# Attention and a state-space convolution on one core: the start of the program in another order, and one planner constant moved from 26 to 26.7

## The chip, the cores and the metric

One core of a Trainium2 chip runs the whole program. The metric is the device time of one execution in microseconds (us). Five engines work side by side, each through its own list of instructions: TensorE (PE, with its weight loads as PEld), VectorE (DVE), ScalarE (ACT), GpSimd (POOL) and SyncE (SP, which issues most DMAs; ACT issues a few).

## The reference

```python
x = A_x                                            # 1 x 2048 x 512, bf16
g = sigmoid((x * gate_w).sum(-1, keepdims=True))
# a: attention, 32 heads of 16
qkv = (x @ wqkv).reshape(B, S, 3, H, Dh)           # -> q, k, v
p = softmax(einsum("bhqd,bhkd->bhqk", q, k) * Dh**-0.5)
a = einsum("bhqk,bhkd->bhqd", p, v).reshape(B, S, D) @ wo
# b: a diagonal state-space convolution over 2048 steps, 128 states a channel
dt = exp(log_dt)[:, None]
P  = exp((dt * (A_re + 1j * A_im))[:, :, None] * arange(L))
K  = einsum("dn,dnl,dn->dl", Cc, P, dt * Bc).real  # 512 x 2048
b  = causal_conv(x, K) + x * Dskip
return g * a + (1 - g) * b
```

## The kernel before, in words

**Attention.** The scores of one head, 128 keys and 512 queries are a tile; there are 2048 tiles. Three tiles make a group, so that there are 683 groups. `qk(g)` multiplies a group's keys (`KT`) by the queries (`Qm`) into one of two PSUM buffers, `SC[0]` and `SC[1]`, in turn. `ex(g)` is one instruction of ACT that takes the exponential of the buffer into `ET` (or `EX`, for the last groups). For some groups VectorE takes the third tile: one instruction turns the scores into the bits of an approximate exponential (`DZ`), and after four such tiles, called a set, three instructions add constants to these bits (`DU`), whose average is the exponential. ACT's instruction in such a group has 1024 columns and not 1536. `pv` multiplies the exponentials by the values (`VE`) into the PSUM bank `OA`. A fourth PSUM buffer, `MB`, serves all else in turn: the other projections, the convolution's kernel (`T`, `Z`) and its products (`U`, `H`), and the output's projection.

**The order of the work.** Every engine's list is written ahead by a planner in Python (`Prog` with a time for each engine and a cost for each instruction, `Sched` with threads of waiting work). The loop over the groups emits `ex(g)` and `qk(g+1)`, and then fills the time of PE, DVE and SP up to ACT's time with work of the threads that is ready. So whatever changes the planner's times early moves all that follows. Where PE's products of a group fall short of `want` columns, the planner adds products with a tile of zeros (`wm`); they compute nothing. Whether VectorE takes a set is settled in `decide`, which asks `win`:

```python
def win(x):
    slow = done() < KA + (x - KX) / KB
    return next((w for w, (lo, hi, _, gap, *_) in enumerate(WIN) if lo <= x < hi and x >= plan["x"] + (SL if slow else gap)
                 and len(sets) <= (min(x, XR) - RX) / RATE + max(x - XR, 0) / RATE2), None)
```

Here `x` is the group and `done()` counts the finished blocks, of 16, of the convolution's kernel. Where these are behind the line with the slope 1/`KB`, sets come at least `SL` = 9 groups apart. `decide` also asks for an idle share of VectorE by the planner's times.

**The front.** Before the loop stands a fixed order. ACT's queue issues the loads of `x0n` (the first 512 rows of x), `ldt` (log_dt), and the first 128 columns of `Wq` and `Wk`; SP's queue the rest. PE runs nine products of zeros, transposes `x0n` with an identity (16 products; SC and MB to `xT`, four casts, one on ACT and three on DVE), runs `WARM` = 6 products of zeros into OA, and projects the first 512 queries (four products into OA) and the first 512 keys (four into SC[0]). DVE masks the queries (`Qm`) and casts the keys (`KT`). Then `qk(0)`, whose three tiles all have the first 128 keys, and the first exponential follow. Beside this, ACT computes `dt` = exp(`ldt`), and from `bn` = `AimT` x `dt` (DVE) a sine and a cosine (`sb_`, `cb`), for which it loads another table, and the table of the exponential again behind them.

All products are recorded at line 701, the helper `mm`; the exponentials stand at L961, DZ at L982, DU at L996.

Of the kernel before, what the change touches and what calls it, by code (L numbers as in the profile page):

```python
# [10 lines left out]
AF = mybir.ActivationFunctionType  # L11
ALU = mybir.AluOpType

P = 128
S = 2048
D = 512
# [16 lines left out]
FILL = 1550  # L33
FILL2 = 1550
OVER = .3
REST = (14, 0, 1792, 425)
# [21 lines left out]
KX = 100  # L58
SL = 9
YQ = 0  # L60
KB = 26
RX = 100
RATE2 = 5.3
XR = 560
# [72 lines left out]
class Prog:  # L137
# [113 lines left out]
    def op(self, eng, fn, R=(), W=(), c=.1, lat=.085, a=0, cfg=None):  # L251
        if self.cap is not None:
            self.cap.append((self.op, (eng, fn, R, W), dict(c=c, lat=lat, a=a, cfg=cfg)))
            return
        if cfg is not None:
            if cfg != self.cfg:
                c += TURN[cfg]
            self.cfg = cfg
        self.act += a
        self.log.append((self.op, self.q, (eng, fn, R, W)))  # L260
        deps = self._deps(eng, R, W)
        i = self.cnt[eng]
        at = self.tm[eng]
        for s, k in deps.items():
            at = max(at, self.fin[(s, k)] + (.03 if s == eng else .05))
        if eng == "PE" and len(self.pt) + 1 >= self.edge():
            at = max(at, self.land())
        self.tm[eng] = at + c
        if eng == "DVE":
            self.busy += c  # L270
        self.fin[(eng, i)] = at + c + lat
        self.cnt[eng] += 1
        w = self._record(eng, fn, deps, eng, i, R, W)
        if eng == "PE":
            b = self.edge()
            self.pt += [at] * (2 + max(w - 1, 0))
            if len(self.pt) > b:
                self.av.append(max(self.pt[b - LEAD] + F1, self.av[-1] + F2))
        return at + c + lat
# [406 lines left out]
def record(nc, p, B, ins):  # L686
    KT, Qm, VE, ET, OT, ON, Rz = (B[n] for n in ("KT", "Qm", "VE", "ET", "OT", "ON", "Rz"))
    OnT = {3: B["OnT3"]}
    OA, MB = B["OA"], B["MB"]
    SC = [B["SC0"], B["SC1"]]  # L690
    sch = Sched(p)
    op, dma = p.op, p.dma
# [6 lines left out]
    def mm(out, lhsT, rhs, R, W, start=True, stop=True, pos=None, c=MM, a=512, cfg="F"):  # L699
        kw = {} if pos is None else dict(tile_position=pos)  # L700
        op("PE", lambda t: t.matmul(out(), lhsT(), rhs(), start=start, stop=stop, skip_group_check=True, **kw), R, W,  # L701
           c=c, lat=.15, a=a, cfg=cfg)
# [80 lines left out]
    def proj_mm(kind, idx, c, bank, q4, wide=False):  # L783

        b, off, sl = bank
        w = B["Wk" if kind == "K" else "Wq"]
        strips(wide, lambda p, n: b(off, [[1, 512]], p, n), lambda p, n: w(q4 * D + 128 * idx + p, [[1, n]]), lambda: xT(q4 * S + 512 * c, [[1, 512]]),
               [xk(c, q4), (w, idx > 0)], [(b, sl, ('p', kind, idx, c))], q4 == 0, q4 == 3)

    def proj_ev(kind, idx, c, bank):  # L790
        b, off, sl = bank
        if kind == "K":
            o, at, ky = KT, idx * S + 512 * c, (idx, c)
        elif c + idx:
            o, at, ky = B["Qs"], idx % 2 * 512, idx % 2
        else:
            o, at, ky = B["Q"], 0, 0
        op("DVE", lambda v: v.tensor_copy(o(at, [[1, 512]]), b(off, [[1, 512]])), [(b, sl, ('p', kind, idx, c))],  # L798
           [(o, ky)], c=.62)
# [139 lines left out]
    def qk(g):  # L939
        sc = SC[g % 2]  # L940
        n = len(slots(g))
        for i, s in enumerate(slots(g)):
            q, j, b, kt, pi = at_slot(s)
            mm(lambda i=i: sc(512 * i, [[1, 512]]),
               lambda j=j, pi=pi, kt=kt: KT(pi * S + 128 * kt, [[1, 128]], 32 * j, 32),
               lambda j=j, b=b: Qm(512 * (b % 2), [[1, 512]], 32 * j, 32),
               [(KT, (pi, kt // 4)), (Qm, (b % 2, j), b)], [(sc, k, g) for k in (range(min(n, 2)) if i == 0 else [i])], pos=(32 * j, 0),
               c=QUAD if i == 0 else 0, a=128, cfg="R")
            if i == 0 and n == 3 and g % 2 == 0 and sch.now is not None:
                jz = 6 - sum(tiles[s] % 4 for s in slots(g))  # L950
                zero(zbank(), 512, (32 * jz, 0), 32, 128, 0, 128, "R")
# [93 lines left out]
    def key(*ns):  # L1045
        return [(B[n], 0) for n in ns]
# [643 lines left out]
            sch.mark(f"qm{b}")  # L1690


    mb, oa = (MB, 0, 0), (OA, 0, 0)
    for q4 in range(4):
        sc = SC[1] if q4 < 3 else MB
        off = 512 * (q4 % 3)
        sl = q4 % 3
        for i in range(4):
            mm(lambda sc=sc, off=off, i=i: sc(off + 128 * i, [[1, P]]), lambda q4=q4, i=i: x0n(D * i + P * q4, [[1, P]]),
               lambda: idb(0, [[1, P]]), [(x0n, 0), (idb, 0)], [(sc, sl, 'x0')], c=.11)  # L1700
        R, W = [(sc, sl, 'x0')], [(xT, (0, q4))]
        if q4 == 1:
            op("ACT", lambda v, sc=sc, off=off, q4=q4: v.copy(xT(q4 * S, [[1, 512]]), sc(off, [[1, 512]])), R, W, c=.58)
        else:
            op("DVE", lambda v, sc=sc, off=off, q4=q4: v.tensor_copy(xT(q4 * S, [[1, 512]]), sc(off, [[1, 512]])), R, W, c=.62)
    op("ACT", lambda a: a.activation(B["dt"](0, [[1, D]]), B["ldt"](0, [[1, D]]), AF.Exp), key("ldt"), key("dt"), c=.6)
    tt("DVE", full("bn"), full("AimT"), full("dt"), ALU.mult, key("AimT", "dt"), key("bn"), F5)
    op("ACT", lambda a: a.activation(B["sb_"](0, [[1, D]]), B["bn"](0, [[1, D]]), AF.Sin), key("bn"), key("sb_"), c=1.9)
    op("DVE", lambda v: v.scalar_tensor_tensor(B["ba"](0, [[1, D]]), B["bn"](0, [[1, D]]), -1.0, B["bn"](0, [[1, D]]), ALU.mult, ALU.max), key("bn"), key("ba"), c=F5)
    op("ACT", lambda a: a.activation(B["cb"](0, [[1, D]]), B["ba"](0, [[1, D]]), AF.Sin, scale=-1.0,  # L1710
                                     bias=hpi(0, [[1, 1]])), key("ba") + [(hpi, 0)], key("cb"), c=.6)
    for k in range(WARM):
        mm(lambda: OA(0, [[1, 512]]), lambda: wm(0, [[1, 128]]), lambda: wm(0, [[1, 512]]), [(wm, 0)], [(OA, 0, "warm")])
    for q4 in range(4):
        proj_mm("Q", 0, 0, oa, q4, True)
    for q4 in range(4):
        proj_mm("K", 0, 0, (SC[0], 0, 0), q4, True)
    op("DVE", lambda v: v.tensor_scalar(Qm(0, [[1, 512]]), OA(0, [[1, 512]]), msk(0, [[1, 1]]), None, ALU.mult),
       [(OA, 0, ('p', "Q", 0, 0)), (msk, 0)], [(Qm, (0, j), 0) for j in range(4)], c=.66)
    proj_ev("K", 0, 0, (SC[0], 0, 0))  # L1720
    decide(0)
    qk(0)
    proj_ev("Q", 0, 0, oa)
# [17 lines left out]
    for g in range(NG):  # L1741
        p.q = g
        for i in range(2 if g in vec else len(slots(g))):
            if held[g] + i in ring:
                sch.force(f"pv{ring[held[g] + i] // 4}")
            ring[held[g] + i] = tiles[3 * g + i]
        ex(g)
        sch.mark(f"g{g}")
        sch.mark(f"blk{at_slot(3 * g)[2]}")
        if g + 1 < NG:  # L1750
            decide(g + 1)
            need(g + 1)
            if g - 1 in vec:
                sch.force(f"bits{g - 1}")
            sc = SC[(g + 1) % 2]
            while lack >= 256 and bare:
                n = 512 if lack >= 512 else 256
                for j in range(4):
                    zero((sc, [(sc, 0, ("z", g + 1))]), n, (0, 32 * j), 128, 32, n * ZCOL if j == 0 else 0, n // 4, "C", True)
                lack -= n  # L1760
                bare -= 1
            lack += p.act
            qk(g + 1)
            if g + 1 in vec:
                i = sets[vec[g + 1][0]]["old"]
                if i is not None:
                    sch.force(f"dvp{i}")
                sch.add(bits(g + 1), 0)
        t = p.tm["ACT"]
        want = (FILL if g < REST[3] else FILL2) * (t - t0) / 1.335 + min(max(lack, -256), 768)  # L1770
        t0 = t
        sch.rest = g < REST[3] and g % REST[0] < REST[1]
        if sch.rest:
            want = max(want, REST[2])
        sch.fill(t, t + OVER, want)
        lack = want - p.act
        p.act = bare = 0
        while lack >= 256 and p.tm["PE"] < t + OVER and g < NG - 1:
            z = zbank()
            if z is None:  # L1780
                bare = BARE
                break
            n = 512 if lack >= 512 else 256
            for j in range(4):
                zero(z, n, (0, 32 * j), 128, 32, n * ZCOL if j == 0 else 0, n // 4, "C")
            lack -= n
        p.act = 0
# [71 lines left out]
```

## Time and profile before

| | |
|---|---|
| time, median of 3 runs | 786.94 us (786.87 to 787.43) |
| the profiled execution's own time | 787.2 us |
| its span | 785.4 us |
| ACT busy | 768.4 us (98%) |
| DVE busy | 748.7 us (95%) |
| PE busy | 689.5 us (88%) |
| first exponential starts | 11.92 us |
| last exponential ends | 776.56 us |

Times within the profile count from the span's start. Some 1.8 us of the profiled time lie outside its span. A row of the timeline merges like instructions that follow each other: start, length, engine, line, what is written and read, and how many. A line of the chain of waits gives the share of the span that each engine holds on the path that ended last.

### The profile page before, as it was taken

How to read it: one execution, taken by the hardware profiler on the slowest of the kernel's cores; microseconds unless marked ns; L12 is line 12 of the kernel's file. 1: busy time of each engine (PE TensorE's matmuls, PEld its weight loads, DVE VectorE, ACT ScalarE, POOL GpSimd, SP SyncE). 2: the span in 40 equal slices, each digit the busy share in tenths (PEclk: the TensorE clock that was granted, in tenths of full speed). 3: DMA queues.
4: the chain of work that ended last, by engine and by line, in shares of the span. 5: the costliest groups of instructions: out<-in, count | busy, mean ns of one | idle time of the engine just before them, and what ended most of it. 6: DMA issues, size and time to landing. Idle time of an engine off the chain costs nothing.

```text
span 785.4 us, 31633 instructions
## 1 busy us (share of the span) xinstructions
PE 689.5 (88%) x14177; PEld 295.3 (38%) x14177; DVE 748.7 (95%) x1307; ACT 768.4 (98%) x694; POOL 11.5 (1%) x21
## 2 busy tenths in 40 slices
PE   7787778788778999989999899989999999889997
PEld 3233332222224544445444455443444444322222
DVE  7999998999999999999999999999999999899996
ACT  7999999999999999999999999999999999999996
POOL 5000000000000000000000000000000000000000
PEclk9999999999999999999999999999999999999999
DMA  9544212302002677674776664775665588721101
GB/s 201 90 108 89 62 40 92 116 31 59 5 8 53 158 178 189 162 205 105 195 177 178 194 158 111 206 193 165 178 143 140 136 194 210 174 48 32 32 15 35
DMA packets 168425, 95.52 MB, mean 122 GB/s; under 512 B 117729, under 2 KB 148834, under 8 KB 167906
## 3 DMA queue, kind: packets, MB, share of 16 engines
q1 hardware_dynamic: 166274, 92.33, 46.1%
q8 instruction: 111, 1.82, 1.0%
q10 hardware_dynamic: 2016, 1.18, 0.7%
q14 instruction: 24, 0.20, 0.1%
HBM read 63.81 MB, written 19.42 MB: 106 GB/s over the span
## 4 chain that ended last, share of the span: by engine, by line
ACT 91%; PE 4%; DVE 3%; DMA 1%; issue 0%; ACTq 0%; DVEq 0%
ACT ET L961 83%; ACT EX L961 8%; PE SC L701 2%; PE OA L701 1%; PE MB L701 1%; DVE DZ L982 1%; DMA Wk<-in_A_wqkv_dram 1%; DVE DU L996 1%; DVE T L1040 0%; DVE Yst L1497 0%; DVE OT L1016 0%; ACTq L705 0%; DVEq L663 0%; DVE KT L798 0%; DVE Kt L1402 0%
## 5 line engine op out<-in xcount | busy, mean ns | idle before, releaser
L961 ACT ACTIVATE ET<-SC 128x1024 bf16<-128x1024 f32 (+1 forms) x614 | 695.7, 1463 | 4.5 <-PE SC L701 3.3
L701 PE MATMUL SC<-Qm,KT 32*128 32x512 bf16 x2048 | 273.4, 385 | 81.2 <-ACT ET L961 70.6
L982 DVE TENSOR_SCALAR DZ<-SC 128x512 uint16<-128x512 f32 x372 | 248.5, 683 | 13.3 <-PE SC L701 11.3
L996 DVE TENSOR_SCALAR DU<-DZ 128x2048 uint16<-128x2048 uint16 x279 | 183.0, 686 | 0.5
L701 PEld LDWEIGHTS SC<-Qm,KT 32*128 32x128 bf16 x2048 | 70.4, 91 | 275.5 <-ACT ET L961 219.0
L701 PE MATMUL OA<-wm 128*32 128x256 bf16 (+3 forms) x862 | 157.3, 340 | 1.2 <-DVE wm L754 1.2
L701 PE MATMUL OA<-ET,VE 128*32 128x512 bf16 x1516 | 158.1, 390 | 0.2
L701 PE MATMUL OA<-DU,VE 128*32 128x512 bf16 x1116 | 105.0, 385 | 0.0
L701 PEld LDWEIGHTS MB<-U,H 128*32 128x32 bf16 x4096 | 83.0, 144 | 22.6 <-issue 11.8
L701 PE MATMUL MB<-U,H 128*32 128x128 bf16 (+7 forms) x4096 | 87.5, 224 | 0.0
L961 ACT ACTIVATE EX<-SC 128x1024 bf16<-128x1024 f32 (+1 forms) x69 | 81.6, 1406 | 0.0
L701 PEld LDWEIGHTS OA<-ET,VE 128*32 128x32 bf16 x1516 | 40.8, 94 | 75.5 <-issue 72.0
L1040 DVE TENSOR_TENSOR T<-B,DT 128x1536 bf16<-128x1536 bf16 x64 | 59.3, 947 | 0.0
L701 PEld LDWEIGHTS MB<-T,Z 128*32 128x32 bf16 x2048 | 46.1, 153 | 12.3 <-issue 7.0
L701 PE MATMUL MB<-T,Z 128*32 128x64 bf16 (+1 forms) x2048 | 48.6, 235 | 0.1
L701 PEld LDWEIGHTS OA<-wm 128*32 128x32 bf16 (+2 forms) x862 | 41.8, 95 | 14.5 <-issue 11.4
L701 PEld LDWEIGHTS OA<-DU,VE 128*32 128x32 bf16 x1116 | 28.8, 96 | 33.9 <-issue 24.2
L701 PE MATMUL OA<-DZ,VE 128*32 128x512 bf16 x372 | 37.2, 384 | 1.0 <-issue 1.0
L1016 DVE STREAM_TRANSPOSE OT<-OA 128x512 f32<-128x512 f32 x32 | 22.7, 709 | 2.8 <-PE OA L701 2.8
L1497 DVE TENSOR_TENSOR Yst<-MB,gt 128x512 bf16<-128x512 f32 x32 | 21.8, 682 | 2.2 <-PE MB L701 1.9
L701 PE MATMUL OA<-EX,VE 128*32 128x512 bf16 x160 | 21.9, 387 | 0.0
L1040 DVE TENSOR_TENSOR ft<-Z,DM 128x1024 bf16<-128x1024 bf16 x32 | 21.3, 676 | 0.0
(145 smaller groups left out, 439.6 us busy)
## 6 DMA issues: line engine op xcount, KB each, us to landing
H<-gm_kd SPq DMA_DIRECT2D x128, 256.0 KB, 3.8
U<-gm_xs SPq DMA_DIRECT2D x128, 134.2 KB, 3.5
T<-B SPq DMA_DIRECT2D x16, 256.0 KB, 3.1
gm_yd<-Yst SPq DMA_DIRECT2D x64, 64.0 KB, 2.9
gm_bd<-B16s SPq DMA_DIRECT2D x3, 1024.0 KB, 4.5
B<-gm_bd SPq DMA_DIRECT2D x12, 256.0 KB, 4.0
gm_kd<-Ks SPq DMA_DIRECT2D x64, 40.0 KB, 3.2
gm_xs<-xP SPq DMA_DIRECT2D x16, 136.0 KB, 3.4
```

The source lines that it names most:

```text
L701: op("PE", lambda t: t.matmul(out(), lhsT(), rhs(), start=start, stop=stop, skip_group_check=True, **kw), R, W, c=c, lat=.15, a=a, cfg=cfg)
L961: op("ACT", lambda a: a.activation(E(at, [[1, 512 * n]]), sc(0, [[1, 512 * n]]), AF.Exp, scale=DH ** -0.5), [(sc, i, g) for i in range(n)] ...
L982: op("DVE", lambda v: v.tensor_scalar(z.u16(512 * k, [[1, 512]]), sc(1024, [[1, 512]]), XS, XB, ALU.mult, ALU.add), [(sc, 2, g)], [(z, k, ...
L996: op("DVE", lambda v, u=u, cut=cut: v.tensor_scalar(u.u16(0, [[1, 2048]]), z.u16(0, [[1, 2048]]), float(cut), None, ALU.add), R, [(u, 0, i ...
L1016: op("DVE", lambda v: v.transpose(OT(512 * w, [[1, 512]]), OA(0, [[1, 512]])), [(OA, 0, b)], [(OT, w, b)], c=.64)
L1040: op(eng, lambda v: v.tensor_tensor(o(), a(), b_(), f), R, W, c=c)
L1497: op("DVE", lambda v, w=w, h=h: v.tensor_tensor(Yst(1024 * w + 4 * h, [[128, R8], [8, 16], [1, 4]]), MB(0, [[1, R8], [R8, 16], [NC, 4]]), ...
```

## The change

It puts the front in another order and changes one constant:

- ACT computes `dt` ahead of its cast of `xT`; PE transposes the second quarter of `x0n` first; DVE computes `bn` ahead of its last cast of `xT`.
- The six products of zeros go from ahead of Q's projection into it, between its third and its fourth product, and write SC[0] in place of OA.
- K's projection writes SC[1] in place of SC[0], in two parts: four products for the keys 0 to 127, four for the keys 128 to 511. DVE casts the first part ahead of `Qm`, and the second behind it. The scores of the keys 128 to 511 wait for the second cast (the new key `'r'`).
- `KB` goes from 26 to 26.7. The choice between `FILL` and `FILL2`, which are both 1550, goes.

```diff
-KB = 26
+KB = 26.7
@@ qk
-               [(KT, (pi, kt // 4)), (Qm, (b % 2, j), b)], ...
+               [(KT, (pi, kt // 4))] + [(KT, 'r')] * (pi == 0 and 0 < kt < 4) + [(Qm, (b % 2, j), b)], ...
@@ front
-    for q4 in range(4):            # transposes and casts of x0n, in one loop
...
-    op("ACT", lambda a: a.activation(B["dt"](0, [[1, D]]), B["ldt"](0, [[1, D]]), AF.Exp), key("ldt"), key("dt"), c=.6)
+    op("ACT", lambda a: a.activation(B["dt"](0, [[1, D]]), B["ldt"](0, [[1, D]]), AF.Exp), key("ldt"), key("dt"), c=.6)
...
+    def k0_mm(q4, sl, at, n):
+        mm(lambda: SC[1](512 * sl, [[1, n]]), lambda: B["Wk"](q4 * D, [[1, P]]), lambda: xT(q4 * S + at, [[1, n]]),
+           [(xT, (0, q4)), (B["Wk"], 0)], [(SC[1], sl, 'k0')], q4 == 0, q4 == 3, c=n / 2000, a=n)
+    for q4 in (1, 0, 2, 3):
+        x0_mm(q4)
+    for q4 in (1, 0, 2):
+        x0_ev(q4)
     tt("DVE", full("bn"), full("AimT"), full("dt"), ALU.mult, key("AimT", "dt"), key("bn"), F5)
     op("ACT", ... sb_ ...)
+    x0_ev(3)
     op("DVE", ... ba ...)
     op("ACT", ... cb ...)
+    for q4 in range(3):
+        proj_mm("Q", 0, 0, oa, q4, True)
     for k in range(WARM):
-        mm(lambda: OA(0, [[1, 512]]), lambda: wm(0, [[1, 128]]), lambda: wm(0, [[1, 512]]), [(wm, 0)], [(OA, 0, "warm")])
+        mm(lambda: SC[0](0, [[1, 512]]), lambda: wm(0, [[1, 128]]), lambda: wm(0, [[1, 512]]), [(wm, 0)], [(SC[0], 0, "warm")])
+    proj_mm("Q", 0, 0, oa, 3, True)
     for q4 in range(4):
-        proj_mm("Q", 0, 0, oa, q4, True)
+        k0_mm(q4, 0, 0, 128)
     for q4 in range(4):
-        proj_mm("K", 0, 0, (SC[0], 0, 0), q4, True)
+        k0_mm(q4, 1, 128, 384)
+    op("DVE", lambda v: v.tensor_copy(KT(0, [[1, 128]]), SC[1](0, [[1, 128]])), [(SC[1], 0, 'k0')], [(KT, (0, 0))], c=.25)
     op("DVE", ... Qm ...)
-    proj_ev("K", 0, 0, (SC[0], 0, 0))
+    op("DVE", lambda v: v.tensor_copy(KT(128, [[1, 384]]), SC[1](512, [[1, 384]])), [(SC[1], 1, 'k0')], [(KT, 'r')], c=.48)
@@ loop over the groups
-        want = (FILL if g < REST[3] else FILL2) * (t - t0) / 1.335 + min(max(lack, -256), 768)
+        want = FILL * (t - t0) / 1.335 + min(max(lack, -256), 768)
```

How the lists of the engines change is seen at three places. The first is PE's list in the front; `idb` is the identity, `wm` the zeros, and `-` is before, `+` is after.

```order
 L701 MATMUL SC<-idb,x0n 128x128 x12
 L701 MATMUL MB<-idb,x0n 128x128 x4
-L701 MATMUL OA<-wm 128x512 x6
-L701 MATMUL OA<-xT,Wq 128x512 x4
-L701 MATMUL SC<-xT,Wk 128x512 x4
+L701 MATMUL OA<-xT,Wq 128x512 x3
+L701 MATMUL SC<-wm 128x512 x6
+L701 MATMUL OA<-xT,Wq 128x512
+L701 MATMUL SC<-xT,Wk 128x128 x4
+L701 MATMUL SC<-xT,Wk 128x384 x4
 L701 MATMUL SC<-Qm,KT 128x512 x6
```

The zeros moved behind three of Q's four products, and K's projection fell into two.

The second is DVE's list at the same place, from the mask's end (`msk`) to the unmasked copy of the queries (`Q`).

```order
 L768 TENSOR_SCALAR msk<-msk 128x1
-L1705 CAST xT<-SC 128x512 x2
-L1705 CAST xT<-MB 128x512
+L1708 CAST xT<-SC 128x512 x2
 L1040 TENSOR_TENSOR bn<-AimT,dt 128x512
-L1709 SCALAR_TENSOR_TENSOR ba<-bn 128x512
-L1718 TENSOR_SCALAR Qm<-OA,msk 128x512
-L798 CAST KT<-SC 128x512
+L1708 CAST xT<-MB 128x512
+L1721 SCALAR_TENSOR_TENSOR ba<-bn 128x512
+L1733 CAST KT<-SC 128x128
+L1734 TENSOR_SCALAR Qm<-OA,msk 128x512
+L1736 CAST KT<-SC 128x384
 L798 CAST Q<-OA 128x512
```

`bn` moved ahead of the last cast of `xT`, and `Qm` behind the first cast of the keys.

The third is ACT's list in the middle of the program, after eight exponentials of 1536 columns that both have. Before:

```order
L961 ACTIVATE ET<-SC 128x1536 x8
L961 ACTIVATE ET<-SC 128x1024 x4
L961 ACTIVATE ET<-SC 128x1536 x4
L961 ACTIVATE ET<-SC 128x1024 x4
L961 ACTIVATE ET<-SC 128x1536 x4
L961 ACTIVATE ET<-SC 128x1024 x4
L961 ACTIVATE ET<-SC 128x1536
```

And of the change, from the same place on:

```order
L961 ACTIVATE ET<-SC 128x1536 x8
L961 ACTIVATE ET<-SC 128x1024 x4
L961 ACTIVATE ET<-SC 128x1536
L961 ACTIVATE ET<-SC 128x1024 x4
L961 ACTIVATE ET<-SC 128x1536
L961 ACTIVATE ET<-SC 128x1024 x4
L961 ACTIVATE ET<-SC 128x1536 x7
```

The sets (the runs of four with 1024 columns) stand elsewhere from here on. Over the whole program there were 372 DZ instructions, 279 DU, 310 exponentials of 1536 columns and 373 of 1024; now there are 368, 276, 314 and 369. The products with zeros went from 950 to 925. SP issues the same DMAs in number, and in the front in the same order.

More of the change, by code (lines that the diff above doesn't have):

```diff
@@ L946, in qk @@
                lambda j=j, b=b: Qm(512 * (b % 2), [[1, 512]], 32 * j, 32),
-               [(KT, (pi, kt // 4)), (Qm, (b % 2, j), b)], [(sc, k, g) for k in (range(min(n, 2)) if i == 0 else [i])], pos=(32 * j, 0),
+               [(KT, (pi, kt // 4))] + [(KT, 'r')] * (pi == 0 and 0 < kt < 4) + [(Qm, (b % 2, j), b)], [(sc, k, g) for k in (range(min(n, 2)) if i == 0 else [i])], pos=(32 * j, 0),
                c=QUAD if i == 0 else 0, a=128, cfg="R")
@@ L1690, in qms, with x0_mm, x0_ev @@
             sch.mark(f"qm{b}")
-    mb, oa = (MB, 0, 0), (OA, 0, 0)
-    for q4 in range(4):
-        sc = SC[1] if q4 < 3 else MB
-        off = 512 * (q4 % 3)
-        sl = q4 % 3
+    oa = (OA, 0, 0)
+    op("ACT", lambda a: a.activation(B["dt"](0, [[1, D]]), B["ldt"](0, [[1, D]]), AF.Exp), key("ldt"), key("dt"), c=.6)
+    def x0_mm(q4):
+        sc, off = (SC[1], 512 * q4) if q4 < 3 else (MB, 0)
         for i in range(4):
             mm(lambda sc=sc, off=off, i=i: sc(off + 128 * i, [[1, P]]), lambda q4=q4, i=i: x0n(D * i + P * q4, [[1, P]]),
-               lambda: idb(0, [[1, P]]), [(x0n, 0), (idb, 0)], [(sc, sl, 'x0')], c=.11)
-        R, W = [(sc, sl, 'x0')], [(xT, (0, q4))]
+               lambda: idb(0, [[1, P]]), [(x0n, 0), (idb, 0)], [(sc, q4 % 3, 'x0')], c=.11)
+    def x0_ev(q4):
+        sc, off = (SC[1], 512 * q4) if q4 < 3 else (MB, 0)
+        R, W = [(sc, q4 % 3, 'x0')], [(xT, (0, q4))]
         if q4 == 1:
-            op("ACT", lambda v, sc=sc, off=off, q4=q4: v.copy(xT(q4 * S, [[1, 512]]), sc(off, [[1, 512]])), R, W, c=.58)
+            op("ACT", lambda v: v.copy(xT(q4 * S, [[1, 512]]), sc(off, [[1, 512]])), R, W, c=.58)
         else:
-            op("DVE", lambda v, sc=sc, off=off, q4=q4: v.tensor_copy(xT(q4 * S, [[1, 512]]), sc(off, [[1, 512]])), R, W, c=.62)
-    op("ACT", lambda a: a.activation(B["dt"](0, [[1, D]]), B["ldt"](0, [[1, D]]), AF.Exp), key("ldt"), key("dt"), c=.6)
+            op("DVE", lambda v: v.tensor_copy(xT(q4 * S, [[1, 512]]), sc(off, [[1, 512]])), R, W, c=.62)
+    def k0_mm(q4, sl, at, n):
[5 more added lines that the diff above has]
+        x0_ev(q4)
     tt("DVE", full("bn"), full("AimT"), full("dt"), ALU.mult, key("AimT", "dt"), key("bn"), F5)
     op("ACT", lambda a: a.activation(B["sb_"](0, [[1, D]]), B["bn"](0, [[1, D]]), AF.Sin), key("bn"), key("sb_"), c=1.9)
+    x0_ev(3)
     op("DVE", lambda v: v.scalar_tensor_tensor(B["ba"](0, [[1, D]]), B["bn"](0, [[1, D]]), -1.0, B["bn"](0, [[1, D]]), ALU.mult, ALU.max), key("bn"), key("ba"), c=F5)
```

## The prediction

> **What bounds the kernel now.** I read the page first: the share of each engine, then the chain of waits.
>
> ```profile
> span 785.4 us, 31633 instructions
> PE 689.5 (88%) x14177; PEld 295.3 (38%) x14177; DVE 748.7 (95%) x1307; ACT 768.4 (98%) x694; POOL 11.5 (1%) x21
> ACT 91%; PE 4%; DVE 3%; DMA 1%; issue 0%; ACTq 0%; DVEq 0%
> ```
>
> ACT is busy for 98% of the span and makes 91% of the chain: the time is the sum of the exponentials, plus what ACT waits, plus the two ends. The groups of ACT by form and its timeline give the sizes.
>
> ```profile
> L961 ACT ACTIVATE ET<-SC 128x1536 bf16<-128x1536 f32 x288 | 414.8, 1720 | 2.4 <-PE SC L701 2.2 <-PE OA L701 0.2
> L961 ACT ACTIVATE ET<-SC 128x1024 bf16<-128x1024 f32 x326 | 330.0, 1236 | 2.1 <-PE SC L701 1.1 <-PE OA L701 0.9
> L961 ACT ACTIVATE EX<-SC 128x1024 bf16<-128x1024 f32 x47 | 51.4, 1270 | 0.0
> L961 ACT ACTIVATE EX<-SC 128x1536 bf16<-128x1536 f32 x22 | 35.1, 1697 | 0.0
> ```
>
> ```profile
> 11.92 1.45 ACT L961 ACTIVATE ET<-SC 128x1536 bf16<-128x1536 f32 x1 [0.89 <-PE SC L701]
> 13.27 0.62 ACT L1098 ACTIVATE ea<-an 128x512 f32<-128x512 f32 x1
> 13.79 69.94 ACT L961 ACTIVATE ET<-SC 128x1536 bf16<-128x1536 f32 x52
> 83.06 0.76 ACT L1542 ACTIVATE ge<-gp 128x16 f32<-128x16 f32 x1
> 83.17 49.01 ACT L961 ACTIVATE ET<-SC 128x1536 bf16<-128x1536 f32 x36
> 132.37 2.79 ACT L961 ACTIVATE ET<-SC 128x1536 bf16<-128x1536 f32 x2 [0.19 <-PE OA L701]
> 135.73 212.69 ACT L961 ACTIVATE ET<-SC 128x1536 bf16<-128x1536 f32 x190 [0.57 <-PE SC L701]
> 772.96 3.60 ACT L961 ACTIVATE EX<-SC 128x1024 bf16<-128x1024 f32 x3
> ```
>
> The 52 wide exponentials from 13.79 to 83.06 follow each other at 69.27 / 52 = 1.332 us. A wide one costs 414.8 / 288 = 1.440 us of busy time and a narrow one 330.0 / 326 = 1.012, so the narrow pace is 0.428 less, 0.904. From the first exponential (11.92) to the end of the last (772.96 + 3.60 = 776.56) are 764.6 us. The 310 wide and 373 narrow ones account for 412.9 + 337.2, and `ea` and `ge` for 0.5 + 0.1, together 750.7. So ACT waits some 13.9 us in this stretch, more than the idle columns show, because short waits hide in the overlap of two exponentials. One place is easily seen: 36 wide ones from 83.17 to 132.37 take 49.20 and not 47.95, and the next two 3.36 and not 2.66, together 1.95 us too long. The stretches of PE with its granted clock say why.
>
> ```profile
> 8.95:12.37 3.42, 2.06 (x38) 1.00 1.11 252
> 128.42:131.83 3.41, 2.06 (x29) 1.00 0.07 11
> 131.83:135.25 3.42, 3.42 (x33) 0.50 0.17 19
> 135.25:138.66 3.41, 3.13 (x50) 1.00 0.19 24
> ```
>
> After a stretch in which PE was busy for 2.06 of 3.41 us, the clock was 0.50 for 3.42 us, and PE could not keep up with ACT.
>
> **The front.** The rows of ACT, DVE and PE from 5 to 12 us, and the landing times:
>
> ```profile
> 1.23 0.52 ACTq L705 DMA_DIRECT2D ldt<-in_B_log_dt_dram  x1
> 5.92 0.58 ACT L1703 CAST xT<-SC 128x512 bf16<-128x512 f32 x1 [1.80 <-PE SC L701]
> 6.56 0.63 ACT L1706 ACTIVATE dt<-ldt 128x512 bf16<-128x512 bf16 x1
> 7.21 1.28 ACT L1708 ACT_TABLE_LOAD   x1
> 9.75 1.28 ACT L961 ACT_TABLE_LOAD   x1
> ...
> 5.00 1.10 PE L701 MATMUL SC<-idb,x0n 128*128 128x128 bf16 x12
> 5.94 0.39 PE L701 MATMUL MB<-idb,x0n 128*128 128x128 bf16 x4
> 6.16 1.46 PE L701 MATMUL OA<-wm 128*128 128x512 bf16 x6
> 8.04 1.04 PE L701 MATMUL OA<-xT,Wq 128*128 128x512 bf16 x4 [0.42 <-DMA Wq<-in_A_wqkv_dram]
> 9.66 1.04 PE L701 MATMUL SC<-xT,Wk 128*128 128x512 bf16 x4 [0.58 <-DMA Wk<-in_A_wqkv_dram]
> 11.48 0.60 PE L701 MATMUL SC<-Qm,KT 32*128 32x512 bf16 x6 [0.79 <-DVE KT L798]
> 13.43 0.39 PE L701 MATMUL SC<-Qm,KT 32*128 32x512 bf16 x3 [0.33 <-ACT ET L961]
> ...
> 5.67 1.29 DVE L1705 CAST xT<-SC 128x512 bf16<-128x512 f32 x2 [1.09 <-PE SC L701]
> 9.12 0.75 DVE L1718 TENSOR_SCALAR Qm<-OA,msk 128x512 bf16<-128x512 f32 x1 [0.24 <-PE OA L701]
> 10.73 0.69 DVE L798 CAST KT<-SC 128x512 bf16<-128x512 f32 x1 [0.86 <-PE SC L701]
> 11.34 0.68 DVE L798 CAST Q<-OA 128x512 bf16<-128x512 f32 x1
> ```
>
> ```profile
> ldt<-in_B_log_dt_dram ACTq DMA_DIRECT2D x1, 128.0 KB, 5.3
> ```
>
> The first exponential waits for a chain of two loads: Wq lands at 8.04, Wk at 9.66. From Wk on it is K's projection (1.04), the cast (0.69), the scores (0.44 from 11.48 to 11.92): 2.26 us.
>
> **The change part by part.**
>
> *dt first.* log_dt is issued at 1.23 and lands 5.3 us later, at 6.53; `dt` started at 6.56 already. So it gains nothing, and the cast of `xT` on ACT, which ran in the wait for it (5.92 to 6.50), now comes behind, at 7.2 to 7.8. The sine's table follows at 7.8 and not 7.2. DVE's `bn` needs the end of `dt`, 7.19, and comes at about 7.3. The last cast of `xT`, `ba`, the cosine and the table of the exponential slip by some 0.6 us each; that table is there at 11.6 and not 11.03. The first scores, 12.1 below, hide that; without them it would cost the 0.6.
>
> *Zeros within Q's projection.* A product of 512 columns follows the one ahead after (1.46 - 0.39) / 5 = 0.214 us, with 0.39 for one alone. Three products of Q from 8.04 end their issue at 8.68; six of zeros at 9.97, 0.31 after Wk has landed; Q's fourth at 10.18. Before, the zeros ran at 6.16 to 7.62, in the wait for Wq, at no cost. Now they stand between the two loads and outlast that wait.
>
> *The first 128 keys apart.* Twelve transposes with 128 columns took 1.10 us, under 0.09 each. Four such products from 10.18 end at about 10.65, with the last one's drain. The cast of 128 columns lies between two rows of DVE:
>
> ```profile
> L1406 DVE CAST Ks<-Kt 128x256 bf16<-128x256 f32 x32 | 7.7, 283 | 0.0
> L1409 DVE CAST Ks<-Kt 128x64 bf16<-128x64 f32 x16 | 3.0, 187 | 0.0
> ```
>
> I take 0.23. `Qm`, 0.75, ran within the wait for Wk before; now it stands behind this cast in DVE's list, on the path. The scores then start at 10.65 + 0.23 + 0.75 + 0.06 = 11.7 and not 11.48, the first exponential at 12.1: **+0.2 us**. Counted with the overlap of two instructions of DVE (the cast of `Q` starts 0.61 after a cast of 0.69) it is +0.1, without it +0.3. The chain behind Wk alone is now shorter: 0.47 + 0.23 + 0.81 = 1.5 us to the scores where 1.82 passed. So if Wk landed later than Q's fourth product, 0.55 us later than here, the front would gain 0.3: that is the lower end.
>
> *The second cast and its wait.* The cast of the keys 128 to 511 comes behind `Qm`, at 11.6 to 12.2. `qk(1)` waits for it, since it needs SC[1] empty and the keys; behind it in PE's list stand the products of V. The first exponential (1.45) and `ea` hide it, as its result is wanted at 13.8 or later. Without this cover it would cost 0.5. `an`, on which `ea` waits, slips from 12.62 to about 13.4 and stays just ahead of the first exponential's end; I take 0, at most 0.3.
>
> *One set less.* The changed lists hold 368 DZ and not 372, 276 DU and not 279.
>
> ```profile
> L982 DVE TENSOR_SCALAR DZ<-SC 128x512 uint16<-128x512 f32 x372 | 248.5, 683 | 13.3 <-PE SC L701 11.3
> L996 DVE TENSOR_SCALAR DU<-DZ 128x2048 uint16<-128x2048 uint16 x279 | 183.0, 686 | 0.5
> ```
>
> VectorE is spared 4 x 0.683 + 3 x 0.686 = 4.8 us. ACT gets four tiles: four of its 683 exponentials are wide and not narrow, 4 x 0.428 = **+1.7 us** on the engine that bounds. It would be 0 if all four fell into places where ACT waits anyway; ACT waits 13.9 of 764.6 us, so I take all of it.
>
> *Everything behind the front.* The planner starts from other times and the constant is another, so the lists differ from the first groups on; the last groups end in the same pieces, at 0. What ACT waits (13.9) is drawn anew. For less: DVE has less to do. For more: PE gets 925 products of zeros and not 950, so its thin stretches are thinner. I take **no change**, and bound it by -4.8 (all that DVE is spared) and +2.0 (one more stretch like that at 131.83).
>
> Sum against the profiled execution: 787.2 + 0.2 + 1.7 = 789.1. It is 0.26 above the median of the runs, so 788.85 for the median, **788.9 us**, 0.24% more.
>
> *A rule of the clock.* The Trainium skill (TensorE: Matmul & The Clock Gate, "What's actually happening") says that PE's clock falls to half after about 3.4 us of idling, in windows that run free of the kernel. The length agrees with the 3.42 us above; the condition does not, since PE was busy for 2.06 us ahead of it. By the page the new idle time in the front, below, is too short to matter and the sum stays 789.1; by the row at 131.83 it could add the 2 us of the first rival.
>
> **The rivals.**
>
> *The clock drops once more (0.21).* With the zeros gone from 6.16, PE idles from 6.3 to 8.04; in the stretch from 5.5 to 8.95 it has then 0.8 + 0.9 = 1.7 us of work. Against it: 2.06 us passed in the stretch at 8.95 and failed in that at 128.42, so busy time alone doesn't decide. If it drops there, the six zeros take 0.43 each, 1.3 more, and the products of Q and K and the scores some 0.7: +2.0. A thin stretch later costs about the same (1.95). **790.9 us.**
>
> *Wk lands late (0.12).* The front gains 0.3: 787.2 + 1.7 - 0.3 - 0.26 = **788.3**, no change.
>
> *VectorE's relief (0.22), the other side.* DVE is busy for 95% and carries 3% of the chain, 23 us, most of it where sets and the convolution's tables meet. If the dropped set frees it there, the waits for DZ shrink, by up to 4.8: **784.1 us**. From 3.5 us on this decides: 788.85 - 3.5 is 0.2% below 786.94. Against it: the waits named above (1.95 at the clock's drop) are PE's.
>
> **How the numbers follow.** A measurement can tell about 0.2%, 1.57 us, from no change: from 785.4 to 788.5. The forecast has 0.45, its own range is 787.8 to 790.0 (front -0.3 to +0.3, waits 0.8 either way); 0.13 of it lies below 788.5. Faster 0.22; within 0.13 + 0.12 = 0.25; slower 0.32 + 0.21 = 0.53. The range, 784.9 to 791.2, holds all but half of VectorE's relief and two drops of the clock.
>
> **What would show it.** First exponential at 12.1 (right), 11.6 (Wk late), or 13 and later with a clock of 0.50 near 9 us (first rival). The zeros from 8.7 to 10, and `Qm` behind the small cast at 10.9. 314 wide exponentials at 1.332 and 369 narrow at 0.904; what is left between the first and the last is the wait: 13.9 if I am right, 9 or less if VectorE's relief counts. I am wrong if the first scores come ahead of 11.4, or if the waits move by more than 2 us without a drop of the clock.

## The result, and the profile after

The change took 789.17 us in the median (787.83 to 794.87, nine runs), the kernel before 786.87 (784.65 to 787.62) beside it. The ratio is 1.0046, with an interval of 1.0024 to 1.0067: slower by 0.2 to 0.7%. A ratio here is formed from all runs and is not the quotient of the two medians. The forecast was 788.9. The profiled execution took 790.2 us, 3.0 more than that of before.

The page of the change: span, busy time and chain, and the group of DZ.

```profile
span 788.4 us, 31595 instructions
PE 692.4 (88%) x14144; PEld 294.0 (37%) x14144; DVE 744.9 (94%) x1301; ACT 771.0 (98%) x694; POOL 11.4 (1%) x21
ACT 90%; PE 5%; DMA 2%; DVE 1%; issue 0%; DVEq 0%; SPq 0%; ACTq 0%
L982 DVE TENSOR_SCALAR DZ<-SC 128x512 uint16<-128x512 f32 x368 | 246.1, 683 | 18.7 <-PE SC L701 16.7
```

ACT still bounds, and is busy for 2.6 us more. DVE has 3.8 us less to do, yet waits longer ahead of DZ, 18.7 us and not 13.3, because PE brings the scores later. The exponentials by form:

```profile
L961 ACT ACTIVATE ET<-SC 128x1536 bf16<-128x1536 f32 x296 | 422.4, 1659 | 2.5 <-PE SC L701 2.3
L961 ACT ACTIVATE ET<-SC 128x1024 bf16<-128x1024 f32 x315 | 317.4, 1200 | 1.5 <-PE SC L701 1.0 <-PE OA L701 0.3
L961 ACT ACTIVATE EX<-SC 128x1024 bf16<-128x1024 f32 x54 | 58.1, 1217 | 0.4 <-PE SC L701 0.3
L961 ACT ACTIVATE EX<-SC 128x1536 bf16<-128x1536 f32 x18 | 28.8, 1645 | 0.0
```

314 are wide and 369 narrow. The front in the timeline (start, length, engine), ACT first, then PE, then DVE:

```profile
6.47 0.63 ACT L1694 ACTIVATE dt<-ldt 128x512 bf16<-128x512 bf16 x1 [2.34 <-DMA ldt<-in_B_log_dt_dram]
7.00 0.57 ACT L1706 CAST xT<-SC 128x512 bf16<-128x512 f32 x1
10.13 1.28 ACT L961 ACT_TABLE_LOAD   x1
11.51 1.45 ACT L961 ACTIVATE ET<-SC 128x1536 bf16<-128x1536 f32 x1
...
7.47 0.82 PE L701 MATMUL OA<-xT,Wq 128*128 128x512 bf16 x3 [0.67 <-DMA Wq<-in_A_wqkv_dram]
8.13 1.46 PE L701 MATMUL SC<-wm 128*128 128x512 bf16 x6
9.43 0.38 PE L701 MATMUL OA<-xT,Wq 128*128 128x512 bf16 x1
9.64 1.04 PE L701 MATMUL SC<-xT,Wk 128*128 128x128 bf16 x8
11.07 0.86 PE L701 MATMUL SC<-Qm,KT 32*128 32x512 bf16 x6 [0.39 <-DVE Qm L1734]
...
10.07 0.29 DVE L1733 CAST KT<-SC 128x128 bf16<-128x128 f32 x1 [0.88 <-PE SC L701]
10.28 0.74 DVE L1734 TENSOR_SCALAR Qm<-OA,msk 128x512 bf16<-128x512 f32 x1
```

`dt` waits for its load as forecast. The zeros run behind three of Q's products, and `Qm` behind the small cast. The first exponential starts at 11.51, 0.41 ahead of before, since Wq landed at 7.47 and not 8.04 and with it the first scores came at 11.07 and not 11.48; it stands right behind the table, which was there at 11.41.

The method of the prediction (the first exponential's start, the exponentials at 1.332 and 0.904 us with 0.6 for `ea` and `ge`, the rest as wait) puts the profiles side by side, in us. The column of the exponentials is their number times these paces, not a measured time, so what a pace is off stands in the wait. "Lists" are the lists of the engines behind the front.

| kernel | span | first exponential | exponentials | wait of ACT | tail |
|---|---|---|---|---|---|
| before | 785.4 | 11.92 | 750.7 | 13.9 | 8.8 |
| the change | 788.4 | 11.51 | 752.5 | 15.6 | 8.8 |
| its front, lists of before | 783.7 | 11.74 | 750.7 | 12.4 | 8.9 |
| its lists, front of before | 788.5 | 12.00 | 752.5 | 15.2 | 8.8 |
| before with one set less at the end | 785.0 | 11.36 | 752.5 | 12.6 | 8.6 |
| the change with 20 more zeros | 787.6 | 11.59 | 752.5 | 14.8 | 8.8 |
| mended front, zeros at 130 us | 783.7 | 10.66 | 750.7 | 13.5 | 8.8 |

Against before, the change gains 0.4 in front, loses 1.8 by the exponentials and 1.7 by waits. The first waits of the change lie where before has none. ACT in the change, behind the front:

```profile
13.38 5.46 ACT L961 ACTIVATE ET<-SC 128x1536 bf16<-128x1536 f32 x4
19.40 6.82 ACT L961 ACTIVATE ET<-SC 128x1536 bf16<-128x1536 f32 x5 [0.56 <-PE SC L701]
27.06 2.79 ACT L961 ACTIVATE ET<-SC 128x1536 bf16<-128x1536 f32 x2 [0.83 <-PE SC L701]
30.35 56.53 ACT L961 ACTIVATE ET<-SC 128x1536 bf16<-128x1536 f32 x42 [0.50 <-PE SC L701]
```

Four wide ones take 6.02 and not 5.33, five take 7.66 and not 6.66, two 3.29 and not 2.66: 2.3 us too long by 30.35. What PE and DVE do there:

```profile
14.88 0.61 PE L701 MATMUL SC<-wm 128*32 128x512 bf16 x8 [1.47 <-ACT ET L961]
...
17.78 0.39 PE L701 MATMUL MB<-xT,Wk 128*32 128x512 bf16 x4
18.97 0.39 PE L701 MATMUL SC<-Qm,KT 32*128 32x512 bf16 x2 [0.48 <-DVE KT L798]
23.59 0.39 PE L701 MATMUL SC<-Qm,KT 32*128 32x512 bf16 x3
24.14 0.39 PE L701 MATMUL MB<-xT,Wk 128*32 128x512 bf16 x4
26.28 0.40 PE L701 MATMUL OA<-ET,VE 128*32 128x512 bf16 x4 [1.75 <-ACT ET L961]
26.62 0.67 PE L701 MATMUL SC<-Qm,KT 32*128 32x512 bf16 x5
...
18.22 0.69 DVE L798 CAST KT<-MB 128x512 bf16<-128x512 f32 x1 [0.63 <-PE MB L701]
24.77 0.68 DVE L798 CAST KT<-MB 128x512 bf16<-128x512 f32 x1
```

Before, at the same place:

```profile
26.02 0.39 PE L701 MATMUL SC<-Qm,KT 32*128 32x512 bf16 x3 [0.17 <-ACT ET L961]
26.34 0.40 PE L701 MATMUL OA<-ET,VE 128*32 128x512 bf16 x4
...
15.25 0.68 DVE L798 CAST KT<-MB 128x512 bf16<-128x512 f32 x1
```

The next block of keys is cast at 18.22 and not at 15.25, and the scores at 18.97 wait for it: ahead of this block's projection, which ran at 13.99 before, PE's list now has products of zeros that wait 1.47 us for an exponential. The block after that is cast by 25.45, but its scores stand in PE's list behind a product `OA<-ET,VE` that waits for an exponential until 26.28: PE idles 1.75 us, and then ACT waits 0.83 for the scores. Before has the scores first (26.02) and that product behind them. The stretches of PE (busy time, granted clock) show what follows:

```profile
23.89:27.30 3.41, 1.66 (x28) 0.96 0.24 37
27.31:30.72 3.41, 3.41 (x84) 0.54 0.02 5
30.72:34.13 3.41, 3.21 (x70) 1.00 0.08 19
```

After a stretch with 1.66 us of work PE ran at about half the clock for another.

### The profile page after: what moved, and what is told of

It reads as the page before. It is cut to its first block, busy times and chain, and to the rows that moved or that the text cites. A ratio compares the mean times of both kernels' runs of the same rounds, so it can differ in the third digit from the quotient of the medians.

```text
span 788.4 us, 31595 instructions
## 1 busy us (share of the span) xinstructions
PE 692.4 (88%) x14144; PEld 294.0 (37%) x14144; DVE 744.9 (94%) x1301; ACT 771.0 (98%) x694; POOL 11.4 (1%) x21
## 3 DMA queue, kind: packets, MB, share of 16 engines
q8 instruction: 111, 1.82, 1.0%
## 4 chain that ended last, share of the span: by engine, by line
ACT 90%; PE 5%; DMA 2%; DVE 1%; issue 0%; DVEq 0%; SPq 0%; ACTq 0%
ACT ET L961 81%; ACT EX L961 8%; PE SC L701 2%; DMA H<-gm_kd 2%; PE MB L701 2%; PE OA L701 1%; DMA Wq<-in_A_wqkv_dram 1%; DVE KT L798 0%; DVE DZ L982 0%; SPq L1516 0%; ACTq L705 0%; DVE T L1040 0%; DVE ft L1040 0%; DVEq L663 0%; DVE OT L1016 0%
## 5 line engine op out<-in xcount | busy, mean ns | idle before, releaser
L982 DVE TENSOR_SCALAR DZ<-SC 128x512 uint16<-128x512 f32 x368 | 246.1, 683 | 18.7 <-PE SC L701 16.7
L996 DVE TENSOR_SCALAR DU<-DZ 128x2048 uint16<-128x2048 uint16 x276 | 181.0, 685 | 0.6
L701 PE MATMUL OA<-wm 128*32 128x256 bf16 (+3 forms) x827 | 154.0, 344 | 1.2 <-DVE wm L754 1.2
L701 PE MATMUL MB<-U,H 128*32 128x128 bf16 (+7 forms) x4096 | 89.3, 224 | 3.2 <-DMA H<-gm_kd 2.8
L701 PE MATMUL OA<-EX,VE 128*32 128x512 bf16 x162 | 24.0, 386 | 0.2 <-ACT ET L961 0.2
```

Of the source, the lines that this page charges most:

```text
L982: op("DVE", lambda v: v.tensor_scalar(z.u16(512 * k, [[1, 512]]), sc(1024, [[1, 512]]), XS, XB, ALU.mult, ALU.add), [(sc, 2, g)], [(z, k, ...
L996: op("DVE", lambda v, u=u, cut=cut: v.tensor_scalar(u.u16(0, [[1, 2048]]), z.u16(0, [[1, 2048]]), float(cut), None, ALU.add), R, [(u, 0, i ...
```

## The experiments

**The front of the change, the lists of before.** The planner runs with the front of before and `KB` = 26, so that every list behind the front is that of before word for word; then the front's recorded instructions are replaced.

```diff
+    n0 = len(p.log)
+    front_old()
+    n1 = len(p.log)
...
+    p.cap = []
+    front_new()
+    p.log[n0:n1] = [(x[0], -1, x[1]) for x in p.cap]
```

> The changed front (order, zeros within Q's projection, keys in two parts) and behind it the lists of before, word for word, with 93 sets. Theory (the time is lost in the lists, not in the front): the first exponential starts at 11.5 to 12.1 where before has it at 11.9 or later, and the time is that of before, -0.4 to +0.3 us. Rival (the front loses, by PE's idle time ahead of Q and a drop of the clock): slower than before by 1.5 us or more, with a granted clock of 0.50 near 9 us. Four more products stand ahead of the old list; they are taken as nothing.

Measured: 786.37 us beside 786.66, ratio 1.0000 (0.9987 to 1.0012). ACT in its profile:

```profile
11.74 1.45 ACT L961 ACTIVATE ET<-SC 128x1536 bf16<-128x1536 f32 x1 [0.35 <-PE SC L701]
13.60 69.94 ACT L961 ACTIVATE ET<-SC 128x1536 bf16<-128x1536 f32 x52
82.99 57.19 ACT L961 ACTIVATE ET<-SC 128x1536 bf16<-128x1536 f32 x42
```

52 exponentials without a wait, as in before. The new front by itself makes no difference that these runs can tell; by the interval it is worth between -1.0 and +0.9 us.

**The front of before, the lists of the change.** The same with the two fronts exchanged and `KB` = 26.7.

```diff
+    front_new()
...
+    p.cap = []
+    front_old()
```

> The front of before and behind it the lists of the change, word for word, with 92 sets. Theory (lists): slower than before by 2.0 to 2.8 us, 1.7 of it four wider exponentials and the rest waits. Rival (front): the time of before within 0.5 us, since only the front of the change loses.

Measured: 790.54 us beside the same 786.66, ratio 1.0045 (1.0029 to 1.0061): the whole loss of the change. ACT:

```profile
13.87 5.46 ACT L961 ACTIVATE ET<-SC 128x1536 bf16<-128x1536 f32 x4
19.89 6.82 ACT L961 ACTIVATE ET<-SC 128x1536 bf16<-128x1536 f32 x5 [0.56 <-PE SC L701]
27.54 2.79 ACT L961 ACTIVATE ET<-SC 128x1536 bf16<-128x1536 f32 x2 [0.83 <-PE SC L701]
```

The waits of 0.56 and 0.83 are those of the change to the hundredth. The 3.9 us in the median lie above the 2.0 to 2.8 that the theory expected. So the loss belongs to the lists, not to the order of the front's own instructions.

**The constant alone.** The change with `KB` = 26, and before with `KB` = 26.7.

```diff
-KB = 26.7
+KB = 26
```

> The change with the constant at 26. It also has 92 sets, in another order, and 968 products of zeros where the change has 925. Theory (one set less costs 1.7, waits and drops of the clock are drawn anew with each list): slower than before by 1.7 us and what its own drops of the clock cost, so +1 to +4. Rival (the constant loses): the time of before within 0.5 us.

```diff
-KB = 26
+KB = 26.7
```

> The kernel before with the constant at 26.7; it has 92 sets and 949 products of zeros. Theory (one set less costs 1.7): slower than before by +1 to +4 us, though its front is the old one. Rival (the new front's lists are what loses): the time of before within 0.5 us.

Measured: 791.65 us, ratio 1.0063 (1.0039 to 1.0087), and 793.81, ratio 1.0088 (1.0060 to 1.0116). Both have 92 sets like the change, where before has 93; their waits are 15.2 and 18.5 us. The times lie 5.0 and 7.2 us above 786.66, both more than the +1 to +4 expected. So neither half of the change is good by itself: each redraws the lists, and all three drawings lose a set and, by the profile, wait longer than before. Of the three, the pair that the change chose has the lowest ratio, though the intervals overlap.

**The price of one set.** Before, with the sets stopped at 92; the lists are those of before up to the last six groups.

```diff
+    MAXSETS = 92
-            if kt < DVK - 1 and win(x) is not None and ...
+            if kt < DVK - 1 and len(sets) < MAXSETS and win(x) is not None and ...
```

> The kernel before with its last set, the 93rd, left to ACT; all lists are those of before up to the last six of 683 groups. Theory (a set less is four wide exponentials for narrow ones, 4 x 0.428): 1.7 us slower than before, with 314 wide and 369 narrow ones and the same wait, 13 to 14 us. Rival (ACT's widths are hidden, only the order of the lists costs): the time of before within 0.5 us.

Measured: 787.82 us beside 786.50, 1.3 more, ratio 1.0013 (1.0000 to 1.0026). Its profile has 314 wide exponentials, as in the change, ACT is busy for 770.0 us where before has 768.4, and waits 12.6 us. So the set costs about what it was counted at, and a third of the 3.9 us that the lists of the change cost above; the interval allows 0 to 2.0 us, so that the runs alone don't exclude the rival.

**Zeros against the drop of the clock.** The change with 20 products of zeros in PE's list at about 24.5 us, in the gap of 1.75 us.

```diff
+            for j in range(4):
+                mm(lambda j=j: OA(0, [[1, 512]], 32 * j, 32), lambda: wm(0, [[1, 32]]), lambda: wm(0, [[1, 512]]), [(wm, 0)], [(OA, 0, tag)], new, new, pos=(0, 32 * j))
...
+    zeros_after(9, 5)
```

> The change with 20 more products of zeros (five times 512 columns in four strips, 1.1 us) in PE's list at the place where it sat idle from 24.5 to 26.3 us ahead of the clock's drop. Theory (the drop at 27 us comes of that idle time and costs 1.6 us in the runs in which it comes): no drop there, the mean granted clock is higher, and the median falls by 0.5 to 1.6 us against the change, to some 788. Rival (the clock falls on its own, or its drop costs nothing): the clock and the time of the change.

Its stretches of PE:

```profile
23.89:27.30 3.41, 2.74 (x50) 1.00 0.26 42
27.31:30.72 3.41, 3.00 (x95) 1.00 0.02 5
```

With 2.74 us of work and not 1.66, the clock stays at 1.00 behind it. The wait of 0.50 that the change has at 30.35 is gone, and 44 wide ones follow each other. But the time is 789.51 us, ratio 1.0042 (1.0029 to 1.0056), and not some 788: no gain shows against the 789.17 of the change. The wait of 0.83 for the scores stays, since they still stand behind the same product. The filled gap goes with a clock that stays up in the profiled run; that this drop costs the change its time is not borne out. Nor is it excluded: the change did not run beside it on this chip, and its repeat below, on another, has 791.47.

In this profile and in that of the first experiment the clock does not fall between the first and the last exponential. ACT waits 14.8 us in this one, with the lists of the change and 20 zeros, and 12.4 in the other, with those of before. So some 2.4 us of waits come with these lists at the full clock.

**A mended front on the lists of before.** The zeros stay ahead of Q, and `Qm` ahead of the keys, as in before; only K's projection and its cast are split in 128 and 384 keys, as in the change.

```diff
-    for q4 in range(4):
-        proj_mm("K", 0, 0, (SC[0], 0, 0), q4, True)
+        for at, n, sl in ((0, 128, 0), (128, 384, 1)):
+            for q4 in range(4):
+                mm(lambda sl=sl, n=n: SC[1](512 * sl, [[1, n]]), ...)
     op("DVE", ... Qm ...)
-    proj_ev("K", 0, 0, (SC[0], 0, 0))
+        op("DVE", lambda v: v.tensor_copy(KT(0, [[1, 128]]), SC[1](0, [[1, 128]])), ...)
+        op("DVE", lambda v: v.tensor_copy(KT(128, [[1, 384]]), SC[1](512, [[1, 384]])), ...)
```

> The front of before, and only the keys in two parts; zeros stay ahead of Q, and the mask of the queries stays ahead of the first cast of the keys. Behind it the lists of before. Theory (the split shortens the chain behind the load of Wk from 1.8 to 0.8 us, and the change spent that on the zeros and on the mask): first exponential at 10.9 to 11.2, held then by the table load, and 0.6 to 1.0 us faster than before. Rival (the front is not on the path, the lists take up any gain): the time of before.

Measured: 785.94 us beside 786.50, ratio 0.9994 (0.9982 to 1.0006). The 0.6 to 1.0 us expected are not shown. In its profile Wk took 7.6 us, the first exponential waited for the scores and started at 11.32, and the clock fell at 12 and at 132 us. The same with 12 products of zeros at 130 us, where before loses its clock:

```diff
+    zeros_after(88, 3)
```

> As the run before in this list, with 12 more products of zeros (0.64 us) in PE's idle time at 130.0 to 130.9 us, ahead of the clock's drop at 131.83 in the profile of before. Theory (that drop comes of the idle time): no drop at 131, and 0.3 to 1.0 us less in the median than without them, as the drop comes in some runs only. Rival: no difference, since the window's phase decides and other thin places take its part.

Measured: 785.73 us beside the same 786.50, ratio 0.9993 (0.9981 to 1.0004). Its profile shows no drop at 131 us; but neither does that of the first experiment, which has these lists without the 12 zeros. And once more, on another chip:

> The mended front with the old lists and the 12 zeros at 130 us, once more, beside the change and before on one chip. If it beats both: 0.5 to 1.0 us below before, with a mean granted clock of 0.999, and 3 us or more below the change. If its lead was chance: the time of before within 0.3 us.

Measured: 785.48 us beside 786.58, ratio 0.9988 (0.9975 to 1.0001). Its front:

```profile
9.37 1.28 ACT L961 ACT_TABLE_LOAD   x1
10.66 1.45 ACT L961 ACTIVATE ET<-SC 128x1536 bf16<-128x1536 f32 x1
...
9.06 1.05 PE L701 MATMUL SC<-xT,Wk 128*128 128x128 bf16 x8 [0.90 <-DMA Wk<-in_A_wqkv_dram]
10.04 0.39 PE L701 MATMUL SC<-Qm,KT 32*128 32x512 bf16 x3
```

From Wk's landing to the first scores pass 0.98 us, where 1.82 passed in before. Here the first exponential waits for the table, not for the scores: it starts right at the table load's end. So the split does what the change wants of it, where `Qm` and the zeros stay out of the path; but it uncovers the table, and what is left, 0.6, 0.8 and 1.1 us in the three medians, is at the edge of what the runs tell. This version is the fastest of all that ran; that it beats the kernel before is not shown, that it beats the change is, as the intervals do not overlap.

**`ldt` loaded ahead.** The mended front with the load of log_dt issued ahead of `x0n`, so that `dt` and with it the table come earlier.

```diff
-    load("ACT", B["x0n"], ...)
     load("ACT", B["ldt"], ...)
+    load("ACT", B["x0n"], ...)
```

> As the mended front with the old lists and the 12 zeros at 130 us, and log_dt's load (128 KB) issued ahead of that of x (512 KB). Theory (the first exponential of the mended front waits for ACT's own chain of dt, two table loads, sine and cosine, which begins when log_dt lands at 6.5): log_dt lands 0.5 us or more earlier, the table is there before 11.0, and the first exponential starts at 10.6 to 11.2, so 0.3 to 0.6 us less than without it. Rival (the loads share the same transfer engines, so x and Wk come later by as much): no difference or a loss of up to 0.5.

Measured: 789.13 us beside 786.58, ratio 1.0046 (1.0028 to 1.0064). This is a failure, by more than its rival had it:

```profile
15.17 1.45 ACT L961 ACTIVATE ET<-SC 128x1536 bf16<-128x1536 f32 x1 [0.92 <-PE SC L701]
8.10 1.46 PE L701 MATMUL SC<-idb,x0n 128*128 128x128 bf16 x12 [2.90 <-DMA x0n<-in_A_x_dram]
9.78 2.77 PE L701 MATMUL OA<-wm 128*128 128x512 bf16 x6
```

```profile
x0n<-in_A_x_dram ACTq DMA_DIRECT2D x1, 512.0 KB, 6.9
```

`x0n` lands 6.9 us after its issue, and not 4.1 to 4.6 as in the other runs. PE, idle for 2.90 us until 8.10, then takes 2.77 us for the six zeros that took 1.46, though the granted clock of that stretch reads 1.00; why they are slower stays open. And `dt` gains nothing, since in this front it stands in ACT's list behind the cast of `xT`, which needs `x0n`.

**The change again**, beside the mended front and on its chip, without an edit.

> The change as it is, once more, for its time and its clock beside the others on one chip. Theory (one set, 1.7 us; the front about 0; waits of its lists, among them drops of the clock): 2 to 4 us above before in the median, with a mean granted clock of 0.995 to 0.997 where before has 0.998. If its drops of the clock were chance: 1.5 to 2 us above, at the clock of before.

Measured: 791.47 us beside 786.58, ratio 1.0060 (1.0041 to 1.0080). The sign stands; the size went from 2.3 to 4.9 us, and this median lies 0.3 us above the upper end of the forecast's range and outside the 2 to 4 us expected here. Its profile shows drops of the clock from 16, 77 and 87 us on, and 16.4 us of waits; behind the first of them an exponential waits 1.97 us for its scores, where the change's first profile has 0.56. The mean granted clock of its runs was 0.9942, of before beside it 0.9979.

## Why the prediction was right, step by step

The sign was right, and so was the term of the set. That the time came within 0.3 us is in part luck: the change's nine runs spread over 7 us, the interval of the ratio stands for 1.9 to 5.3 us where the forecast has 2.0, and the repeat gave 4.9. The front's term is too small for these runs to tell, and the waits were sized too small.

*dt first.* As forecast: `dt` waited for its load until 6.47 (forecast 6.56), and the table came at 11.41 (11.6). That the first scores hide the table held in the profile of the change by 0.1 us only.

*The front, +0.2.* The step from Wq's landing to the first scores was forecast at 11.7 - 8.04 = 3.7 us and measured 11.07 - 7.47 = 3.6. The small cast took 0.29 and not 0.23. What the step took as fixed was not: Wq landed 0.57 earlier in this profile, so the front gained 0.41 where +0.2 stood; 0.57 - 0.41 is the 0.2 that it would have cost with the landings of before. The landings of Wq and Wk move more from run to run than the reordering is worth, and in the first experiment the front's price was 0 within 0.13%, 1 us, which neither shows nor excludes +0.2. The prediction named first scores ahead of 11.4 as a sign that it is wrong, and a first exponential at 11.6 as the sign of a late Wk. They came at 11.07 and 11.51, and neither meant that: both signs took Wq's landing as fixed.

*The second cast.* Hidden, as forecast.

*One set less, +1.7.* Borne out: with the last set alone left out, ACT is busy for 1.6 us more and the median is 1.3 higher (interval 0 to 2.0). The 752.5 - 750.7 = 1.8 of the table is the same count at the same paces and no test of it.

*Waits unchanged.* This was the mis-sized term: taken as 0, it was +1.7 in the profile, inside its bounds (-4.8 to +2.0), and +2.5 in the repeat's, outside them. The profile of before that it is counted against holds a drop of the clock, at which ACT lost 1.95. The lists alone, set included, cost 3.9 us in the median; with 1.3 to 1.7 for the set, 2.2 to 2.6 belong to the drawing of the lists. Where: in the first 31 us, 2.3 us of waits that before hasn't, since the keys come later and scores stand behind a product that waits for ACT. The prediction looked for the price at the places of the front and of the sets and did not follow the changed lists from 13 to 31 us, where it could have read that order. That these waits are the price is read from the profiles; no run moved those scores ahead of that product.

*The clock drops once more.* Right in kind, wrong in place. There was no drop near 9 us; in two of the three profiles of these lists without added zeros, the change's and that with the old front, there is one at 27, behind the thin stretch that the lists made, and in the repeat there are three elsewhere. Over the 33 runs of the first nine, the old front and the added zeros, all with these lists, a clock lower by 0.001 goes with 0.5 us more (correlation 0.79), and at the full clock they come to 788.5, where before comes to 786.0 over the 76 runs beside all experiments; the six runs of the repeat, added, leave this as it is. So most of the loss is there at the full clock, and by this fit some 1.1 us goes with the lower clock. This is a correlation, and the experiment that took one drop away does not decide it, so the share stays open.

The Trainium skill (TensorE: Matmul & The Clock Gate, "What's actually happening") has the clock fall after an idle window. The measurement differs: PE was busy for 1.66 of 3.41 us ahead of the drop at 27 us, and with 2.74 us of work there was none in the one profile taken.

*VectorE's relief.* This rival went the wrong way: busy for 3.8 us less, DVE waited 5.4 us longer ahead of DZ, and 16.7 of its 18.7 us there ended with PE's scores. So DVE did not hold ACT at those places.

*Wk lands late.* Wk was there before Q's fourth product ended, so this did not happen in the change's profile. The mended front, where `Qm` is off that path, shows the shorter chain that this rival spoke of: 0.98 us.

What stays open: how much of the loss is the clock's; and why these lists draw more drops in some runs than in others.

## What to carry to other kernels

In a program whose lists are drawn by a planner, a change at the start is two changes: its own instructions, here worth no more than 1 us either way, and the redrawing of all that follows, 3.9 us here. Replay the old lists behind the new start to tell them apart, and read the new lists at the first groups, above all for products that stand behind one that waits for the bounding engine. A saving of a few tenths on a path that starts with a load is smaller than the spread of the load's landing.

## What the runs showed of the hardware

The landings of the change, and their spread:

```profile
ldt<-in_B_log_dt_dram ACTq DMA_DIRECT2D x1, 128.0 KB, 5.2
Wq<-in_A_wqkv_dram ACTq DMA_DIRECT2D x1, 128.0 KB, 5.6
Wk<-in_A_wqkv_dram ACTq DMA_DIRECT2D x1, 128.0 KB, 6.5
```

Wk's load, issued at 2.3 us in the same order, took from 6.5 us here to 7.6 us with the mended front; in the profiles in which a product waited for it, that product started from 9.06 to 9.90 us. One load of 128 KB issued ahead of `x0n` delayed its landing by more than 2 us in the one profile taken (6.9 us after its issue, and not 4.1 to 4.6). And the clock fell behind stretches in which PE was busy for half of the time or somewhat more (1.66 of 3.41 us in the change, 2.06 in before). The same work doesn't always bring the drop; with the front of the change and the lists of before the stretches of PE were:

```profile
128.42:131.83 3.41, 2.06 (x30) 1.00 0.07 11
131.83:135.25 3.42, 2.96 (x51) 1.00 0.25 29
```

Again 2.06 us of work, and the clock stayed at 1.00 behind it.
